# First pair's tiles, the shared block's place, the order of bc and den, and the last pair's DMAs in an attention and two-MoE kernel

## The chip, the cores and the metric

The kernel runs on one core of a Trainium2 chip. The metric is device time in microseconds (us) of one execution. A core has a matrix engine (PE), a vector engine (DVE), a scalar engine (ACT), GpSimd (POOL) and a queue engine (SP) that issues DMAs; each runs its own instructions in the order in which they stand.

## What is computed

Softmax attention with a tanh cap over 24 heads of 448 rows and 64 columns, then two feed-forward blocks on the 896 x 768 result. The weights come as 64-bit floats, the rest as 32-bit floats.

```python
scores = scale * np.matmul(q, k.transpose(0, 1, 3, 2))
scores = cap * np.tanh(scores / cap)
scores = scores - np.max(scores, axis=-1, keepdims=True)
attn = np.exp(scores)
attn = attn / (np.sum(attn, axis=-1, keepdims=True) + 1e-09)
x = np.matmul(attn, v)                      # then (B*S, H*D) = (896, 768)
h = x @ w_in;  g = np.where(h > 0.0, h, np.exp(np.minimum(h, 0.0)) - 1.0);  x = g @ w_out
h = np.maximum(x @ w_in2, 0.0);  out = h * h @ w_out2
```

## The kernel before, in words

**Pairs.** The 24 heads are worked in 12 pairs; two pairs are a group, and rows are loaded a group at a time (`load_group`: k, q, v, and "w", the last 64 rows of v). A pair's k and q are transposed on PE into one PSUM tile `pt` (`turn`, L177), which ACT copies to a rounded high part (`high`) and DVE subtracts to a low part `kql` (`low`, L189); `pt` has one buffer, so `turn(n + 2)` follows `low(n + 1)`. Every product of two matrices is then three matmuls on these parts. 448 rows are three blocks of 128 and one of 64. Scores of blocks 0 to 2 (`scores`, L230) contract over 64 rows, and the two heads run side by side in the upper and lower 64 rows of PE; block 3 of both heads is one matmul over 128 rows. ACT makes tanh (L239) and exp; `split_p` splits the result into `ph` and `pl` on DVE (L258, L259); `pv` (L281) multiplies with v, part 0 for four blocks, part 1 for the other two and, at its end, the "shared" block of the last 64 rows, whose two heads again sit in 64 rows each and which is plain 32-bit. The columns of ones beside v give the sums. `pv_out` copies the result to `pvs` (ACT, L290) and asks for the row of sums, `den` (DMA, L293). `norm` takes the reciprocal, writes it to DRAM (`far`, L305) and reads it back spread over 64 rows (`bc`, L310). `norm_x` multiplies (`xn`, L323) and splits into `xh` (L329) and `xl` (L330). The steps of one pair are spread over three turns of the loop: turn n has scores of pair n and n + 1, `pv` of n - 1 and n, `norm(n - 2)` and `norm_x(n - 3)`.

**Weights.** `Stream` turns 64-bit pieces (`wst`, five buffers) into `wf`, then `wh` and `wl`. Per piece that is an abs (ACT L385, or DVE L381 when the stream is "alone"), two DVE steps (clamp L394, shift L398), two more (sign L419, low L426, which also asks for the next piece), a copy (ACT L439, or DVE) and a subtraction (`rest`, DVE L434). `advance` interleaves the steps of two pieces. Before, pieces 0 and 1 are converted on DVE in front of the pair loop, interleaved, with piece 2 opened between; the pieces from 2 on come when the loop is done.

**The front.** `first_pair` transposes pair 0 in three pieces (k blocks 0 to 2; q; k's last block) into the one tile `pt`, with idle matmuls (`warm`, L217) between, and ACT and DVE take each piece in turn.

**The tail.** After the loop the first feed-forward matmuls (`mm_in`; b = 0 and 1 are the batches, the last pairs are b = 1) run between the last pairs' steps. `late_kc` tells how many of the 2 x 6 (k chunk, batch) steps of the first two accumulators are written ahead of the last pair's `norm_x`; the others stand behind it.

**Order.** All is written by hand (`manual_schedule`); instructions stand on their engine in the order of the code. SP issues nearly all DMAs, one after the other; an issue that waits holds up all behind it.

Of the kernel before, what the change touches and what calls it, by code (L numbers as in the profile page):

```python
# [26 lines left out]
def attention_moe_kernel(  # L27
# [133 lines left out]

    def turn(n, pieces=REST):
        if n >= len(pairs):
            return
        g, pp = divmod(n, 2)
        hs = slice(2 * pp, 2 * pp + 2)
        if ("pt", n) not in st:
            st["pt", n] = ps1.tile([P, 2, W], F32, name="pt", tag="pt")
        for u, cs in pieces:
            for c in range(NFULL + 1)[cs]:  # L170
                if c < NFULL:
                    src = nat[g]["kq"[u]][:, c, hs].rearrange("p h d -> p (h d)")
                elif u == 0:
                    src = kzs[g % 2][:, pp]
                else:
                    src = qzs[g % 2][:, hs].rearrange("p h d -> p (h d)")
                nc.tensor.transpose(st["pt", n][:, u, c * P:(c + 1) * P], src, ident)  # L177
# [15 lines left out]
    def first_pair():  # L193
        warm(5)
        cut = [(u, slice(cs.start * P, cs.stop * P)) for u, cs in FIRST]
        st["qk", 0] = [ap_.tile([P, 2, W], F32R, name=x, tag=x) for x in ("kqh", "kql")]
        h, l = st["qk", 0]
        for piece, (u, cs) in zip(FIRST, cut):
            turn(0, (piece,))
            warm(2)  # L200
            nc.scalar.copy(h[:, u, cs], st["pt", 0][:, u, cs])
            if piece is not FIRST[2]:
                nc.vector.tensor_tensor(
                    l[:, u, cs], st["pt", 0][:, u, cs], h[:, u, cs].bitcast(F32),
                    op=ALU.subtract,
                )
        u, cs = cut[2]
        nc.vector.tensor_tensor(
            l[:, u, cs], st["pt", 0][:, u, cs], h[:, u, cs].bitcast(F32), op=ALU.subtract
        )  # L210

    def warm(n):

        if "warm" not in st:
            st["warm"] = ps1.tile([P, 2, W], F32, name="po", tag="po")
# [121 lines left out]
    class Stream:  # L337
# [66 lines left out]
        def end(self, i):  # L404
# [19 lines left out]
            def low():  # L424
# [342 lines left out]
```

## Time and profile before

| what | us |
|---|---|
| median of 3 runs (611.66 to 614.39) | 612.2 |
| profiled execution, its own time | 610.04 |
| its span, first to last instruction | 608.3 |
| PE busy in the span | 587.9 (97%) |
| DVE / ACT / POOL busy | 429.1 (71%) / 334.9 (55%) / 55.7 (9%) |

The span begins at 0. Pairs run to about 138 us, the two feed-forward blocks from there to the end. PE is idle for 20 us in all, nearly all of it before 151 us. A busy time of PE is no proof that PE is at its peak: the clock that it is granted stands in a column of its own, and matmuls of one shape can be compared by how far apart they start.

### The profile page before, as it was taken

The page shows a single profiled execution, that of the slowest core. Times are in us where ns is not written, and L with a number is a line of the kernel's source. Part 1 is how long each engine was busy: PE and PEld are TensorE (multiplying, and loading weights), DVE is VectorE, ACT ScalarE, POOL GpSimd, SP SyncE. Part 2 cuts the span into 40 slices and gives each one's busy share as a digit, 9 for nine tenths or more (in the row PEclk, how much of TensorE's full clock was granted, in tenths as well). Part 3 has the DMA queues.
Part 4 walks back from the last instruction along what each step waited for, and adds up shares of the span by engine and source line. Part 5 has one row for each costly group of instructions (what it writes and reads, how often), then busy time and mean ns, then how long its engine had stood idle before and what let it go on. Part 6 is the DMA issues. An engine that isn't in the chain of part 4 may idle for free.

```text
span 608.3 us, 8606 instructions
## 1 busy us (share of the span) xinstructions
PE 587.9 (97%) x3040; PEld 526.2 (87%) x3040; DVE 429.1 (71%) x833; ACT 334.9 (55%) x484; POOL 55.7 (9%) x80
## 2 busy tenths in 40 slices
PE   7599999998999999999999999999999999999997
PEld 6477667676999999999999999999999999999997
DVE  2658999987999888676665666676777779991000
ACT  2579888852888777643333334656666655541000
POOL 3134323301000000000000000000000012130000
PEclk9799999999999999999999999999999999999999
DMA  7752441013444433333333244333334446632000
GB/s 189 192 129 68 103 111 37 28 32 109 130 133 132 126 105 96 96 112 110 99 113 121 89 128 130 105 108 118 113 107 117 108 115 188 183 92 103 23 24 35
DMA packets 82844, 64.76 MB, mean 106 GB/s; under 512 B 38512, under 2 KB 78704, under 8 KB 82800
## 3 DMA queue, kind: packets, MB, share of 16 engines
q1 hardware_dynamic: 80800, 63.74, 35.9%
q10 hardware_dynamic: 2000, 0.46, 0.3%
q8 instruction: 24, 0.39, 0.3%
q14 instruction: 20, 0.16, 0.1%
HBM read 61.34 MB, written 2.80 MB: 105 GB/s over the span
## 4 chain that ended last, share of the span: by engine, by line
PE 88%; DMA 4%; ACT 3%; DVE 2%; SPq 1%; issue 1%; ACTq 0%; POOL 0%; DVEq 0%
PE acc L497 19%; PE acc L498 19%; PE acc L496 19%; PE po L281 9%; PE acc L698 7%; PE acc L699 6%; PE acc L697 6%; PE sc L230 4%; ACT pvs L290 2%; ACT e L239 1%; DMA bc<-far 1%; DMA far<-rd 1%; DMA q<-in_q_dram 1%; DMA v<-in_v_dram 1%; DMA wst<-in_moe_w_in_dram 1%
## 5 line engine op out<-in xcount | busy, mean ns | idle before, releaser
L496 PE MATMUL acc<-xh,wh 128*128 128x448 f32 x384 | 139.9, 364 | 2.3 <-ACT xh L329 2.3
L497 PE MATMUL acc<-xl,wh 128*128 128x448 f32 x384 | 139.9, 364 | 0.2 <-DVE xl L330 0.2
L498 PE MATMUL acc<-xh,wl 128*128 128x448 f32 x384 | 139.6, 364 | 0.0
L439 ACT CAST wh<-wf 128x384 fp32r<-128x384 f32 (+2 forms) x114 | 57.9, 508 | 104.0 <-PE acc L497 85.4
L385 ACT ACTIVATE wf<-wst 128x384 f32<-128x384 f32 (+2 forms) x130 | 70.5, 543 | 62.0 <-DVE wl L434 35.1
L434 DVE TENSOR_TENSOR wl<-wf,wh 128x384 fp32r<-128x384 f32 (+2 forms) x116 | 63.7, 549 | 56.0 <-ACT wh L439 55.9
L496 PEld LDWEIGHTS acc<-xh,wh 128*128 128x128 f32 x384 | 72.1, 188 | 9.1 <-ACT xh L329 2.7
L498 PEld LDWEIGHTS acc<-xh,wl 128*128 128x128 f32 x384 | 72.1, 188 | 5.7 <-DVE wl L434 0.5
L497 PEld LDWEIGHTS acc<-xl,wh 128*128 128x128 f32 x384 | 72.1, 188 | 5.5 <-DVE xl L330 0.5
L426 DVE SCALAR_TENSOR_TENSOR wf<-wst,wf 128x384 uint32<-128x384 uint32 (+3 forms) x132 | 71.2, 540 | 0.0
L419 DVE SCALAR_TENSOR_TENSOR wf<-wst,wf 128x384 uint32<-128x384 uint32 (+3 forms) x132 | 71.2, 539 | 0.0
L497 PE MATMUL acc<-gl,wh 128*128 128x448 f32 x192 | 70.0, 365 | 0.0
L498 PE MATMUL acc<-gh,wl 128*128 128x448 f32 x192 | 70.0, 364 | 0.0
L496 PE MATMUL acc<-gh,wh 128*128 128x448 f32 x192 | 69.8, 364 | 0.0
L398 DVE TENSOR_SCALAR wf<-wf 128x384 uint32<-128x384 uint32 (+3 forms) x132 | 54.6, 414 | 0.6
L394 DVE TENSOR_SCALAR wf<-wf 128x384 f32<-128x384 f32 (+3 forms) x132 | 48.1, 364 | 7.1 <-ACT wf L385 7.1
L434 POOL TENSOR_TENSOR late<-wf,late 128x336 fp32r<-128x336 f32 x16 | 15.2, 950 | 387.9 <-ACT late L439 387.9
L239 ACT ACTIVATE e<-sc,tsc 128x896 f32<-128x896 f32 (+1 forms) x48 | 42.4, 915 | 8.8 <-PE sc L230 8.7
L684 DVE COPY o<-acc 128x432 f32<-128x432 f32 (+1 forms) x8 | 4.5, 558 | 53.9 <-PE acc L699 47.5
L698 PE MATMUL acc<-wl,gh 128*128 128x432 f32 x112 | 40.3, 359 | 0.0
L699 PE MATMUL acc<-wh,gl 128*128 128x432 f32 x112 | 40.1, 358 | 0.0
L697 PE MATMUL acc<-wh,gh 128*128 128x432 f32 x112 | 40.0, 357 | 0.0
(83 smaller groups left out, 984.0 us busy)
## 6 DMA issues: line engine op xcount, KB each, us to landing
wst<-in_moe_w_in_dram SPq DMA_DIRECT2D x64, 384.0 KB, 3.2
wst<-in_moe_w_out_dram SPq DMA_DIRECT2D x24, 384.0 KB, 3.3
wst<-in_moe_w_out_dram SPq DMA_DIRECT2D x16, 432.0 KB, 3.3
wst<-in_moe_w_out_dram SPq DMA_DIRECT2D x16, 336.0 KB, 3.0
wst<-in_moe_w_out_dram SPq DMA_DIRECT2D x12, 256.0 KB, 2.6
bc<-far SPq DMA_DIRECT2D x24, 112.0 KB, 2.8
k<-in_k_dram SPq DMA_DIRECT2D x18, 128.0 KB, 2.9
v<-in_v_dram SPq DMA_DIRECT2D x24, 96.0 KB, 2.8
```

What stands on the lines that cost most here:

```text
L281: nc.tensor.matmul(po[:, u, :S], vt[r, at[0]], pt[r, at[1]], start=i == 0 and j < 2, stop=i == 1 and j >= len(mms) - 2,)
L385: nc.scalar.activation(self.f[i], hi.bitcast(F32), AF.Abs)
L419: v.scalar_tensor_tensor(out=fb, in0=hi, scalar=0xC0000000, in1=fb, op0=ALU.bitwise_and, op1=ALU.bitwise_or,)
L426: v.scalar_tensor_tensor(out=fb, in0=lo, scalar=29, in1=fb, op0=ALU.logical_shift_right, op1=ALU.bitwise_or,)
L434: (v if dst is None else nc.gpsimd).tensor_tensor(wl, self.f[i], wh.bitcast(F32), op=ALU.subtract)
L439: (v.tensor_copy if self.alone else nc.scalar.copy)(wh, self.f[i])
L496: nc.tensor.matmul(acc, w[0], x[0], start=first, stop=False)
L497: nc.tensor.matmul(acc, w[0], x[1], start=False, stop=False)
L498: nc.tensor.matmul(acc, w[1], x[0], start=False, stop=last)
L697: nc.tensor.matmul(acc, gh[:, f, gs], w[0], start=a, stop=False)
L698: nc.tensor.matmul(acc, gh[:, f, gs], w[1], start=False, stop=False)
L699: nc.tensor.matmul(acc, gl[:, f, gs], w[0], start=False, stop=z)
```

## The change

- **The first pair.** The three pieces of pair 0 get a PSUM tile each (`pt`, `po`, and one of the two `sc`), the idle matmuls write to the other `sc`. The copies of all three pieces stand together on ACT, the subtractions on DVE, and the two small steps on `tsc` follow them. Eight idle matmuls stand in front instead of five, two behind the first piece, none behind the second and six behind the third.
- **Loads in front.** k and q of group 0 are loaded pair by pair: pair 0's first (k on SP, q on ACT), pair 1's behind them, then v of pair 0, two weight pieces, v of pair 1, and only then group 1. The first weight piece is asked for by ACT.
- **First weight pieces.** Piece 0 is converted as a whole in front of the loop (`whole`), piece 1 as a whole behind `split_p(0, 0)`.
- **The shared block** stands first in `pv` part 1.
- **bc ahead of den.** `norm(n - 2)` is written ahead of `pv_out(n - 1)`.
- **The last pair.** `start` (abs of pieces 2 and 3, clamp and shift of 2) moves into the last turn of the loop, one `advance` ahead of `split_p(11, 1)`, and the others are spread. Asking for new pieces is held (`held`) until the last `norm_x` is written. `late_kc` is 10 instead of 8. The subtraction `xl` of pairs 9 and 10 is on DVE, not POOL.

```diff
-    FIRST = ((0, slice(0, NFULL)), (1, slice(0, NFULL + 1)), (0, slice(NFULL, NFULL + 1)))
...
     def first_pair():
-        warm(5)
...
+        idle = psc.tile([P, 2, W], F32, name="sc", tag="sc")
+
+        def warm(n):
+            for _ in range(n):
+                nc.tensor.matmul(idle[:, 0, :P], ident, ident, start=True, stop=True)
+
+        qk = [ap_.tile([P, 2, W], F32R, name=x, tag=x) for x in ("kqh", "kql")]
+        st["qk", 0] = qk
+        warm(8)
+        pieces = []
+        for u, cs, pool, tag, after in (
+            (0, range(NFULL), ps1, "pt", 2),
+            (1, range(NFULL + 1), ps1, "po", 0),
+            (0, range(NFULL, NFULL + 1), psc, "sc", 6),
+        ):
+            t = pool.tile([P, 2, W], F32, name=tag, tag=tag)
+            at = slice(cs[0] * P, (cs[-1] + 1) * P)
+            for c in cs:
+                turn_one(t[:, u, c * P:(c + 1) * P], 0, u, c)
+            warm(after)
+            pieces.append((t[:, u, at], *(x[:, u, at] for x in qk)))
+        for t, h, l in pieces:
+            nc.scalar.copy(h, t)
+        for t, h, l in pieces:
+            nc.vector.tensor_tensor(l, t, h.bitcast(F32), op=ALU.subtract)
...
         if i == 1:
             shared = vss[n // 2 % 2], st["e", n]
-            mms += [(u, r, None, shared) for u, r in enumerate(ROWS)]
+            mms = [(u, r, None, shared) for u, r in enumerate(ROWS)] + mms
...
-    def norm_x(n, copy=nc.vector.tensor_copy, low=nc.gpsimd):
+    def norm_x(n, copy=nc.vector.tensor_copy):
...
-                if not self.alone:
-                    self.load()
+                self.hold += 1
+                if not (self.alone or self.held):
+                    self.release()
...
+        def release(self):
+            self.held = False
+            while self.hold:
+                self.hold -= 1
+                self.load()
...
+        def whole(self):
+
+            self.alone = True
+            self.open(self.done)
+            emit(self.begin(self.done) + self.end(self.done))
+            self.done += 1
+            self.alone = False
...
-        load_group(0, "k")
-        load_group(0, "q", dma=nc.scalar.dma_start)
+        load_group(0, "k", 0)
+        load_group(0, "q", 0, dma=nc.scalar.dma_start)
         nc.scalar.dma_start(capt, cap.unsqueeze(0).to_broadcast([P, 1]))
+        ws.load(nc.scalar.dma_start)
+        load_group(0, "kq", 1)
+        load_group(0, "vw", 0)
+        fill_kq(1, nc.gpsimd)
         ws.load()
         ws.load()
-        load_group(0, "vw", 0)
-        fill_kq(1, nc.gpsimd)
+        load_group(0, "vw", 1)
         load_group(1, "kq")
-        load_group(0, "vw", 1)
-        for _ in range(3):
-            ws.load()
+        ws.load()
+        ws.load()
         load_group(1, "vw")
...
-        emit(ws.start())
-        emit(ws.advance())
-        emit(ws.advance())
-        ws.settle()
+        ws.whole()
         for n in range(np_):
...
             turn(n + 2)
+            norm(n - 2)
+            if last:
+                emit(ws.start())
             pv_out(n - 1)
-            norm(n - 2)
...
+            if n == 0:
+                ws.whole()
             if n == 1:
-                ws.load()
-                ws.load()
+                ws.release()
...
-        late_kc = 2 * (KC - 2)
+        late_kc = 2 * (KC - 1)
+        ws.held = True
+        emit(ws.advance())
         split_p(np_ - 1, 1)
...
-        emit(norm_x(np_ - 1, nc.scalar.copy, nc.vector))
+        x, x_high, x_low = norm_x(np_ - 1, nc.scalar.copy)
+        x()
+        x_high()
+        ws.settle()
+        x_low()
+        ws.release()
```

SP at the start of the program, before. k, kz and q, qz are the full blocks and the last 64 rows of k and q (kz_90, qz_92 of group 0, kz_91, qz_93 of group 1), v and vs the same of v, wst a weight piece:

```order
L118 DMA k<-in_k_dram 128x4x64 x3
L127 DMA kz_90<-in_k_dram 64x2x64 x2
L366 DMA wst<-in_moe_w_in_dram 128x3x128 x2
L133 DMA v<-in_v_dram 128x3x64 x2
L139 DMA vs_98<-in_v_dram 64x64 x2
L118 DMA k<-in_k_dram 128x4x64 x3
L127 DMA kz_91<-in_k_dram 64x2x64 x2
L118 DMA q<-in_q_dram 128x4x64 x3
L122 DMA qz_93<-in_q_dram 64x4x64
```

The same place now:

```order
L118 DMA k<-in_k_dram 128x2x64 x3
L127 DMA kz_90<-in_k_dram 64x64 x2
L118 DMA k<-in_k_dram 128x2x64 x3
L127 DMA kz_90<-in_k_dram 64x64 x2
L118 DMA q<-in_q_dram 128x2x64 x3
L122 DMA qz_92<-in_q_dram 64x2x64
L133 DMA v<-in_v_dram 128x3x64 x2
L139 DMA vs_98<-in_v_dram 64x64 x2
L371 DMA wst<-in_moe_w_in_dram 128x3x128 x2
...
L127 DMA kz_91<-in_k_dram 64x2x64 x2
L118 DMA q<-in_q_dram 128x4x64 x3
L122 DMA qz_93<-in_q_dram 64x4x64
```

Group 1's last DMA (qz_93), for which the transposes of pair 2 wait, was the 20th that SP issues and is now the 33rd.

PE around `pv` part 1 of a pair, before (the first row is the last of block 2's scores, e with vs_98 is the shared block, the last row is the first of block 3's scores):

```order
L230 MATMUL sc<-kqh,kql 128x448 x2
L281 MATMUL po<-ph,vh_94 128x448 x2
L281 MATMUL po<-ph,vl_96 128x448 x2
L281 MATMUL po<-pl,vh_94 128x448 x2
L281 MATMUL po<-e,vs_98 128x448 x2
L230 MATMUL sc<-kqh 128x448
```

and now:

```order
L232 MATMUL sc<-kqh,kql 128x448 x2
L284 MATMUL po<-e,vs_98 128x448 x2
L284 MATMUL po<-ph,vh_94 128x448 x2
L284 MATMUL po<-ph,vl_96 128x448 x2
L284 MATMUL po<-pl,vh_94 128x448 x2
L232 MATMUL sc<-kqh 128x448
```

The shared block, of 64 rows, now follows the scores of block 2, also of 64 rows; the block-3 scores, of 128 rows, follow `pl` with vh, also of 128.

SP at the end of the pairs, before (den of the last pair, then two weight pieces, then far and bc of the last pair):

```order
L293 DMA den<-pvs 64x1x14
L366 DMA wst<-in_moe_w_in_dram 128x3x128 x2
L305 DMA far<-rd 64x14
L310 DMA bc<-far 64x448 x2
L366 DMA wst<-in_moe_w_in_dram 128x3x128 x23
```

and now:

```order
L296 DMA den<-pvs 64x1x14
L308 DMA far<-rd 64x14
L313 DMA bc<-far 64x448 x2
L371 DMA wst<-in_moe_w_in_dram 128x3x128 x25
```

The two weight pieces that stood between den and far stand behind bc.

## Rows read from the trace of the kernel before

**Rows 1.** Timeline of PE, 0 to 30 us: start, us, line, operation, [idle before <-releaser]

```profile
25.61 0.90 PE L177 MATMUL pt<-ident,k 128*128 128x128 f32 x3 [6.87 <-DVE kql L189]
...
27.50 0.74 PE L230 MATMUL sc<-kqh 64*128 64x448 f32 x2
...
28.42 0.57 PE L230 MATMUL sc<-kqh,kql 64*128 64x448 f32 x2
28.79 0.57 PE L230 MATMUL sc<-kqh 64*128 64x448 f32 x2
```

**Rows 2.** Timeline of DVE, 0 to 30 us

```profile
19.60 0.36 DVE L381 TENSOR_SCALAR wf<-wst 128x384 uint32<-128x384 uint32 x1 [6.11 <-DMA wst<-in_moe_w_in_dram]
...
24.33 1.22 DVE L189 TENSOR_TENSOR kql<-pt,kqh 128x1024 fp32r<-128x1024 f32 x1
```

**Rows 3.** Timeline of SP, 0 to 40 us

```profile
4.70 0.91 SPq L366 DMA_DIRECT2D wst<-in_moe_w_in_dram  x2
...
23.51 1.26 SPq L127 DMA_DIRECT2D kz<-in_k_dram  x2
```

**Rows 4.** Tile qz, 8 to 16 us: issue of group 1's qz to its landing

```profile
DMA to landing us min/median/max: 2.4/2.4/2.4
```

**Rows 5.** Stretches: length, busy PE, PEld, DVE, ACT, POOL (instructions), PEclk, DMA share, GB/s

```profile
23.60:30.20 6.60, 4.59 (x21) 3.54 (x21) 6.50 (x7) 1.17 (x2) 0.00 (x0) 0.50 0.63 140
30.40:37.00 6.60, 6.60 (x34) 4.71 (x34) 3.35 (x3) 4.16 (x5) 1.97 (x2) 1.00 0.17 39
100.00:120.00 20.00, 19.48 (x110) 13.68 (x109) 19.42 (x24) 17.06 (x17) 6.53 (x11) 1.00 0.10 27
```

**Rows 6.** Timeline of PE, 68.7 to 84.2 us: one pair's part 1

```profile
79.40 0.37 PE L230 MATMUL sc<-kqh,kql 64*128 64x448 f32 x2
79.70 0.67 PE L281 MATMUL po<-ph,vh 128*128 128x448 f32 x2
80.20 0.57 PE L281 MATMUL po<-ph,vl 128*128 128x448 f32 x2
80.61 0.57 PE L281 MATMUL po<-pl,vh 128*128 128x448 f32 x2
81.11 1.02 PE L281 MATMUL po<-e,vs 64*128 64x448 f32 x4
82.07 0.47 PE L230 MATMUL sc<-kqh 128*128 128x448 f32 x1
...
84.08 0.47 PE L230 MATMUL sc<-kqh 64*128 64x448 f32 x2 [0.26 <-ACT e L239]
```

**Rows 7.** Chain that ended last, 60 to 90 us: start, us, what

```profile
82.21 0.91 ACT pvs L290
83.12 0.92 ACT e L239
```

**Rows 8.** Waits of DVE, 60 to 130 us: us in total, times, longest

```profile
DVE xn L323 <- DMA bc<-far: 2.3, 5, 0.5
```

**Rows 9.** Timeline of PE, 131 to 154 us

```profile
150.36 0.47 PE L496 MATMUL acc<-xh,wh 128*128 128x448 f32 x1 [2.34 <-ACT xh L329]
151.02 0.48 PE L497 MATMUL acc<-xl,wh 128*128 128x448 f32 x1 [0.20 <-DVE xl L330]
```

**Rows 10.** Timeline of SP, 130 to 157 us

```profile
134.46 0.48 SPq L305 DMA_DIRECT2D far<-rd  x1
136.16 1.09 SPq L310 DMA_DIRECT2D bc<-far  x2
139.34 0.49 SPq L293 DMA_DIRECT2D den<-pvs  x1
139.93 1.97 SPq L366 DMA_DIRECT2D wst<-in_moe_w_in_dram  x2
142.02 0.47 SPq L305 DMA_DIRECT2D far<-rd  x1
145.48 1.09 SPq L310 DMA_DIRECT2D bc<-far  x2
```

More of the change, by code (lines that the diff above doesn't have):

```diff
@@ L153, in prep_v, with turn_one, turn @@
             nc.gpsimd.tensor_tensor(l, vn, h.bitcast(F32), op=ALU.subtract)
-    FIRST = ((0, slice(0, NFULL)), (1, slice(0, NFULL + 1)), (0, slice(NFULL, NFULL + 1)))
-    REST = ((0, slice(0, NFULL + 1)), (1, slice(0, NFULL + 1)))
-    def turn(n, pieces=REST):
+    def turn_one(to, n, u, c):
+        g, pp = divmod(n, 2)
+        hs = slice(2 * pp, 2 * pp + 2)
+        if c < NFULL:
+            src = nat[g]["kq"[u]][:, c, hs].rearrange("p h d -> p (h d)")
+        elif u == 0:
+            src = kzs[g % 2][:, pp]
+        else:
+            src = qzs[g % 2][:, hs].rearrange("p h d -> p (h d)")
+        nc.tensor.transpose(to, src, ident)
+    def turn(n):
         if n >= len(pairs):
             return
[L165 to L177, printed above, removed]
+        st["pt", n] = pt = ps1.tile([P, 2, W], F32, name="pt", tag="pt")
+        for u in range(2):
+            for c in range(NFULL + 1):
+                turn_one(pt[:, u, c * P:(c + 1) * P], n, u, c)
     def high(n):
@@ L193, in first_pair @@
     def first_pair():
-        warm(5)
[L195 to L215, printed above, removed]
-        for _ in range(n):
-            nc.tensor.matmul(st["warm"][:, 0, :P], ident, ident, start=True, stop=True)
+        idle = psc.tile([P, 2, W], F32, name="sc", tag="sc")
[21 more added lines that the diff above has]
+            nc.vector.tensor_tensor(l, t, h.bitcast(F32), op=ALU.subtract)
     def scores(n, c):
@@ L329, in norm_x @@
             lambda: copy(hi, xn),
-            lambda: low.tensor_tensor(lo, xn, hi.bitcast(F32), op=ALU.subtract),
+            lambda: nc.vector.tensor_tensor(lo, xn, hi.bitcast(F32), op=ALU.subtract),
         ]
@@ L350, in __init__ @@
             self.alone = False
+            self.hold, self.held = 0, False
         def add(self, src, a, n, keys=None, dst=None):
@@ L359, in get, with load @@
             return tuple(t[:, o] for t in self.parts[i])
-        def load(self):
+        def load(self, dma=nc.sync.dma_start):
             i = len(self.loaded)
@@ L562, in attention_moe_kernel @@
             prep_v(n + 1)
-            emit(norm_x(n - 3, low=nc.vector))
+            emit(norm_x(n - 3))
             split_p(n, 0)
@@ L594, in attention_moe_kernel @@
         emit(norm_x(np_ - 3))
-        while ws.done < 4:
-            emit(ws.advance())
+        emit(ws.advance())
         mm_in(0, 0, begun[0], xh, xl, kb[1:7:2])
```

15 lines of the change are left out of this document (6 added, 9 removed).

## The prediction

> **What bounds the kernel now.** I read the table of busy times first: PE is busy 97% of the span, so only PE's idle stretches and the time its matmuls lose can be won, and from about 151 us on PE has next to no idle time. Then the timelines of PE show where the idle time lies, and there are three places.
>
> (a) The front. PE stands 6.87 us and goes on at 25.61, released by `kql` on DVE [rows 1]. DVE had waited 6.11 us, until 19.60, for weight piece 2, then ran the rest of the conversion of pieces 0 and 1, 12 steps, up to 24.33, where `low(1)` starts [rows 2]. That is 4.73 us, 0.39 a step. A weight piece that nobody needs until the pairs are done holds up `low(1)`, and so `pt`, and so PE. Behind the idle time PE ran at half clock: 0.50 in the stretch 23.6 to 30.2, 1.00 in the next [rows 5]. Two pairs of 64-row score matmuls start 0.37 us apart there (28.42 to 28.79) [rows 1]; at full clock matmuls of the same 448 columns start 0.205 apart (80.20 to 80.61 for two) [rows 6].
>
> (b) The pairs. One pair takes about 9.2 us and its chain is PE, then ACT: when `pv` part 1 ends, ACT copies `pvs` (0.91) and makes a tanh (0.92) [rows 7], and only then has PE a free tile for the next scores; PE does block 3 and eight transposes meanwhile and still waits 0.26 [rows 6]. DVE is as full: 19.42 of 20 us [rows 5]; from 60 to 130 us it waits for nothing but `bc`, 2.3 us in all [rows 8].
>
> (c) The tail. PE waits 2.34 us for `xh` of the last pair and then starts the second matmul 0.66 behind the first instead of 0.205, so 0.46 more [rows 9].
>
> **The change part by part.**
>
> *Front loads.* `low(1)` no longer waits for piece 2: piece 0 alone, 7 steps of 0.39 = 2.7 us of DVE, stands in front, its DMA is asked for by ACT early, and piece 1 comes behind `split_p(0, 0)`, where DVE has room (3.35 busy of 6.6 in 30.4 to 37.0 [rows 5]). Without that room it would cost its 2.7 us again. What is late next is the data for pair 2's transposes, which stand in front of pair 1's scores on PE. Their last DMA, qz of group 1, was SP's 20th issue and is now the 33rd. SP's 6th issue starts at 4.70 and its 37th at 23.51 [rows 3], 18.81/31 = 0.607 us each. The 33rd starts at 4.70 + 27 x 0.607 = 21.1 and lands 2.4 later [rows 4], at 23.5; the other seven transposes can be done as their blocks land, so pair 1's scores start near 23.8, against 27.50 [rows 1]: 3.7 us earlier. The own tiles of the pieces, the earlier scores of pair 0 and the changed idle matmuls bring nothing by themselves: all of it is over before 23.5 and lies beside SP's issuing. Were the loads not the limit, they would be worth more; so their cost is 0, with SP's queue as the cover.
>
> The clock takes part of it back. PE stands idle again before 23.5, so I expect half clock again. If full clock comes back at the same time as before, about 30.3, there are 3.7 us more at half clock, in which PE does 0.205/0.37 = 0.55 of the work: 1.65 lost, gain 2.05. If half clock lasts as long after the burst's start as before (25.61 to 30.3), the gain is the whole 3.7. If it lasts a second stretch like 23.6 to 30.2, PE is at half clock for 11 us instead of 2.8 behind the first scores, 8.2 x 0.45 = 3.7 is lost, and the gain is 0. I take **2.0** (the first, since nothing moves the clock's change by itself), bounds 0 and 3.7.
>
> *Shared block.* From 64-row to 128-row matmuls the start-to-start time is 0.30 (79.40 to 79.70) instead of 0.205, and the next two take 0.50 (79.70 to 80.20) instead of 0.41: 0.10 + 0.09, so a change of shape costs about 0.2 us. Before, part 1 had three: scores to `ph`, `pl` to shared (80.61 to 81.11, again 0.50 for two), shared to block 3 (81.11 to 82.07) [rows 6]. Now one is left, shared to `ph`. Of the two that go, one lies on the chain; the other lies between the end of part 1 and the next scores, where PE waits for ACT anyway: it turns into idle time, 0.26 growing to about 0.45. So 0.2 a pair. It holds for the first 11 pairs; the last has other 128-row matmuls around it, two changes before and two now. 11 x 0.2 = 2.2 us.
>
> *DVE and bc.* A faster pair needs a faster DVE. `far` and `bc` no longer queue behind `den`, which waits for ACT's `pvs`, so I expect the 2.3 us of waits [rows 8] to go. `den` now queues behind `far` and `bc`, and behind `den` the loads of k, q and v; its only reader is the reciprocal of the next turn, some 9 us on, so this costs 0; the cover is that turn. In the last turn DVE gets clamp and shift of piece 2, 2 x 0.39 = 0.8, ahead of `split_p(11, 0)`. DVE's room to pair 11 is therefore 2.3 - 0.8 = 1.5, and the 0.4 from the first two pairs, when DVE still waits for ACT: 1.9, less than PE's 2.2. I take **1.9**; bounds 0.5 (the `bc` waits stay in part) and 4.4 (both changes of shape count, 22 x 0.2).
>
> *Last pair's DMAs.* Before, SP issued `den` at 139.34, then two weight pieces until 139.93 + 1.97 = 141.90, then `far` at 142.02; `bc` could go only at 145.48, 3.46 later, while a pair earlier it took 136.16 - 134.46 = 1.70 with no weight piece on the way [rows 10]. Without them `far` can go when the reciprocal is there, at 139.34 + about 1.8 for `den` + 0.3 = 141.4 (1.8 is an estimate from that 1.70, the same kind of small DMA). That is 0.6 + 1.76 = 2.4 earlier, so `xh` at 150.36 - 2.4 = 148.0. PE's work lasted to 150.36 - 2.34 = 148.0, and three matmuls more (`late_kc`) stand in front of the wait, 3 x 0.205 = 0.6, so the wait of 2.34 goes, and most of the 0.46. The steps of piece 2 that now stand ahead of `split_p(11, 1)` lie where DVE waits for exp, and the two `xl` moved to DVE (about 0.5 each, an estimate from 0.39 for 384 columns) lie beside PE's 48 matmuls; uncovered they would cost 1.0. The held weight pieces (7 to 9) land some us later than before; PE needs pieces 4, 5 and 6 first, which are long there, so this costs 0; if it did not hold, PE would wait for `wl` behind the tail. I take **2.6**; bounds 1.2 (`far` as slow as before, only the queue's 0.6 and the three matmuls' 0.6) and 3.3.
>
> **Sum.** 2.0 + 1.9 + 2.6 = 6.5 us. Against the profiled execution's 610.04 that is 603.5; the median of the runs shown lies 2.2 above it, and by the median it is 605.7. I take the middle of the two, 611.1 - 6.5 = **604.6**.
>
> **The rivals.**
> - *Group 1's rows come late.* For it: 13 more issues stand ahead of qz. Against it: the same 0.607 held over 31 issues of all kinds. At 0.74 each qz lands at 27.1, PE starts as before, the gain is 4.5: 606.6. Chance 0.10.
> - *The clock.* The stretch of idle time in front of pair 1's scores is as long as before or longer, and half clock could last through a second stretch: front 0, 606.6. Chance 0.10. The Trainium skill, TensorE: Matmul & The Clock Gate, section "HAM oscillation — how this bites in real kernels", says that a gap between bursts sets PE back to half clock and that this is paid again at each gap; by that rule the front's half clock stays whatever the loads do, and the trace agrees with its 0.50 [rows 5]. The page also has the moment of the change vary from run to run, which would let this rival and the full 3.7 both occur.
> - *The change of shape stays.* Scores are in the rounded format and the shared block is plain 32-bit; no row shows these two side by side in 64 rows. If that change costs the 0.2 that I take out, the pairs gain nothing: 606.5. Chance 0.08. The Trainium skill, TensorEngine Tiling, section "Key Properties", ties the drain to the tiling mode ("Changing tiling mode (not just tile) drains the TensorE"), which speaks against this rival; no run so far shows this pair.
> - *DVE becomes the bound.* It is 97% busy; if `bc` keeps coming late, PE waits for `ph` and `pl` and the pairs give 0.5: 606.0. Chance 0.08.
> - *It doesn't do what it says in the tail.* `far` takes 3.4 us for another reason than the weight pieces: tail 1.2, 606.0. Chance 0.05.
> - *Slower.* SP's front queue is the place, 1 us for each us is the price. If qz of group 1 lands after 27.2, PE starts later than before; slower than before from 27.2 + 4.5 = 31.7, at (31.7 - 2.4 - 4.70)/27 = 0.91 us an issue. At 1.1 it lands at 36.8, and the time is 611.1 + 5.1 = 616.2. For it: many small transfers at once; against it: 0.607 was measured with the DMA engines as full. Chance 0.04.
>
> **How the numbers follow.** The forecast has 0.55, the rivals 0.45 together. A measurement of this kernel can tell about 0.5%, 3.1 us, so faster means under 609.1. Each rival alone but the last stays under it; two or three together don't, for which I count 0.12. Faster 0.84, same 0.12, slower 0.04. The range: the bounds of the three terms give gains from 1.7 to 11.4, but the ends need all three; two terms at the low end and one at its value give 2.0 + 0.5 + 1.2 = 3.7 or less, against the median 608.5; at the high end 3.7 + 1.9 + 3.3 = 8.9 against the profiled 610.04, 601.1.
>
> **What would show it.** Right: no wait of DVE for a weight piece in the first 25 us, PE's transposes of pair 2 released by a DMA near 23.5; pairs of about 9.0 us with 0.30 only behind the shared block and PE's wait for tanh near 0.45; no waits of `xn` for `bc`; `far` to `bc` 1.7 us for the last pair and no wait of PE for `xh` over 0.5. Wrong: qz landing behind 25, half clock beyond 31, the shared block starting 0.30 behind the scores, PE waiting for `ph` or `pl` in each pair, or new waits of PE for `wl` behind 150.

## The result and the profile after

The changed kernel takes 604.49 us (median of 4 runs, 603.58 to 605.78) against 611.93 for the kernel before (4 runs, 610.03 to 614.39): a ratio of 0.9878, 95% interval 0.9838 to 0.9918, so the gain is clear of the noise. The profiled execution took 605.78, its span is 604.0. The forecast was 604.6. PE is busy 582.4 us (96%), DVE 429.7, ACT 334.9, POOL 62.1.

**Front.** PE after, 12 to 36.6 us (start, us, line, operation, [idle before <-releaser]); these answer [rows 1]:

```profile
17.81 1.37 PE L167 MATMUL pt<-ident,k 128*128 128x128 f32 x3 [4.96 <-DMA k<-in_k_dram]
...
24.82 0.45 PE L167 MATMUL pt<-ident,qz 128*128 128x128 f32 x1 [2.16 <-DMA qz<-in_q_dram]
25.20 0.74 PE L232 MATMUL sc<-kqh 64*128 64x448 f32 x2
...
35.95 0.47 PE L232 MATMUL sc<-kqh 64*128 64x448 f32 x2 [0.42 <-ACT e L241]
```

SP after, 15 to 23 us, which answers [rows 3]:

```profile
19.80 0.61 SPq L122 DMA_DIRECT2D qz<-in_q_dram  x1
20.45 1.13 SPq L371 DMA_DIRECT2D wst<-in_moe_w_in_dram  x2
```

The tile qz after, 18 to 26 us, which answers [rows 4]:

```profile
DMA to landing us min/median/max: 4.9/4.9/4.9
```

DVE no longer stands in the way; the rows of group 1 do. qz is issued at 19.80 and lands 4.9 us later, at 24.7, so pair 1's scores begin at 25.20, 2.3 us earlier than before. Pair 2's begin at 35.95, against 37.96 before: a lead of 2.0.

Stretches after (columns as in [rows 5], which they answer):

```profile
17.00:25.00 8.00, 3.35 (x8) 1.46 (x8) 5.55 (x10) 0.00 (x0) 1.97 (x4) 0.50 0.81 203
25.20:29.20 4.00, 4.00 (x17) 3.16 (x17) 0.53 (x1) 2.47 (x3) 0.00 (x0) 0.51 0.76 175
29.40:36.00 6.60, 6.18 (x38) 4.69 (x36) 2.66 (x3) 3.87 (x5) 2.01 (x2) 1.00 0.63 143
...
127.20:131.60 4.40, 4.40 (x14) 3.94 (x15) 4.33 (x7) 1.67 (x3) 0.00 (x0) 0.61 0.00 0
```

PE ran at 0.50 (1.2 GHz) from 17 to 29 us, behind its 4.96 us of idle time, and a second time behind 127.2 us, where before had 1.00.

**Pairs.** PE after, 66 to 81.5 us, one pair's part 1, which answers [rows 6]:

```profile
71.94 0.47 PE L232 MATMUL sc<-kqh 64*128 64x448 f32 x2 [0.42 <-ACT e L241]
...
76.50 0.37 PE L232 MATMUL sc<-kqh,kql 64*128 64x448 f32 x2
76.70 0.92 PE L284 MATMUL po<-e,vs 64*128 64x448 f32 x4
77.55 0.67 PE L284 MATMUL po<-ph,vh 128*128 128x448 f32 x2
78.06 0.57 PE L284 MATMUL po<-ph,vl 128*128 128x448 f32 x2
78.47 0.57 PE L284 MATMUL po<-pl,vh 128*128 128x448 f32 x2
78.88 0.36 PE L232 MATMUL sc<-kqh 128*128 128x448 f32 x1
...
80.94 0.47 PE L232 MATMUL sc<-kqh 64*128 64x448 f32 x2 [0.42 <-ACT e L241]
```

The shared block starts 0.20 behind the scores (76.50 to 76.70), block 3 starts 0.41 behind `pl` for two matmuls, and the period is 80.94 - 71.94 = 9.00 (9.19 to 9.30 before, one pair 9.53).

Waits of DVE after, 60 to 130 us (total, times, longest), which answer [rows 8]:

```profile
DVE wf L399 <- ACT wf L390: 1.2, 1, 1.2
```

The waits for `bc` are gone, and a new one is there.

**Tail.** DVE after, 121 to 131 us:

```profile
122.99 0.36 DVE L399 TENSOR_SCALAR wf<-wf 128x384 f32<-128x384 f32 x1 [1.24 <-ACT wf L390]
123.38 0.36 DVE L403 TENSOR_SCALAR wf<-wf 128x384 uint32<-128x384 uint32 x1
...
125.93 1.08 DVE L260 CAST ph<-e 128x1792 fp32r<-128x1792 f32 x1
```

ACT after, 116 to 128 us:

```profile
120.73 1.79 ACT L249 ACTIVATE e<-e,capt 128x1792 f32<-128x1792 f32 x1
122.43 0.97 ACT L390 ACTIVATE wf<-wst 128x384 f32<-128x384 f32 x2
```

PE after, 120 to 153 us, which answers [rows 9]:

```profile
127.16 1.05 PE L284 MATMUL po<-ph,vh 128*128 128x448 f32 x4 [2.48 <-DVE ph L260]
128.05 1.64 PE L284 MATMUL po<-ph,vl 128*128 128x448 f32 x4
```

PE before, 118 to 131 us, the same matmuls:

```profile
129.71 1.04 PE L281 MATMUL po<-ph,vh 128*128 128x448 f32 x4 [0.28 <-ACT pvs L290]
```

SP after, 128 to 152 us, which answers [rows 10]:

```profile
138.34 0.51 SPq L296 DMA_DIRECT2D den<-pvs  x1
140.43 0.46 SPq L308 DMA_DIRECT2D far<-rd  x1
142.09 1.09 SPq L313 DMA_DIRECT2D bc<-far  x2
```

`start`, now in the last turn, puts clamp and shift of piece 2 ahead of the last pair's split on DVE. The clamp waits for ACT's abs, and the abs stands behind an exp of 1.79 us. So `ph` is 2 us late, PE idles 2.48 us instead of 0.28, and half clock follows it (0.61). The last pair's DMAs did what they should: `far` to `bc` takes 142.09 - 140.43 = 1.66 (3.46 before), and PE's wait of 2.34 for `xh` is gone.

From the 101st matmul of the feed-forward blocks on, all kernels below take 446.6 us to the end of PE's last matmul. So what sets them apart lies in the first 155 us, and this table follows it. Medians are us; the ratio is against the kernel before, run beside it on the same chip; then three starts from the profiled execution.

| kernel | median | ratio (95%) | profiled, own time | pair 2's first scores | pair 4's block 2 | pair 11's first scores |
|---|---|---|---|---|---|---|
| before | 611.93 | | 610.04 | 37.96 | 60.44 | 121.33 |
| after | 604.49 | 0.9878 (0.9838-0.9918) | 605.78 | 35.95 | 57.99 | 116.97 |
| e1_start_late | 603.70 | 0.9859 (0.9834-0.9884) | 603.48 | 34.97 | 57.02 | 115.96 |
| e2_shared_only | 610.18 | 0.9970 (0.9944-0.9996) | 610.93 | 37.99 | 60.06 | 120.22 |
| e3_bc_first | 611.90 | 0.9983 (0.9964-1.0002) | 609.64 | 37.59 | 60.16 | 120.82 |
| e4_front_only | 608.76 | 0.9945 (0.9925-0.9965) | 609.94 | 35.52 | 58.01 | 119.29 |
| e5_tail_only | 608.03 | 0.9949 (0.9930-0.9969) | 608.98 | 38.86 | 62.08 | 122.93 |
| e6_group1_early | 605.68 | 0.9902 (0.9870-0.9933) | 605.64 | 30.81 | 58.59 | 118.13 |
| e7_turn2_late | 604.78 | 0.9896 (0.9861-0.9932) | 603.65 | 29.81 | 57.38 | 116.36 |
| e8_warm | 603.59 | 0.9876 (0.9846-0.9905) | 603.42 | 33.19 | 57.19 | 116.31 |
| e9_shared_and_bc | 608.60 | 0.9944 (0.9924-0.9965) | 608.66 | 38.35 | 60.41 | 119.40 |
| e10_warm_less_sp | 602.55 | 0.9841 (0.9816-0.9866) | 602.60 | 33.45 | 55.50 | 115.56 |
| e11_front_anew | 601.95 | 0.9830 (0.9805-0.9856) | 602.51 | 32.74 | 55.01 | 115.06 |
| e12_front_again | 600.31 | 0.9796 (0.9780-0.9812) | 600.31 | 26.66 | 54.38 | 113.37 |

e1 to e4 ran on one chip (before: 611.82 there), e5 to e8 on another (611.18), e9 to e11 on a third (611.50), e12 on a fourth (612.35). A start read from one trace is good to about 1 us only: at pair 2, kernels whose front is that of before lie between 37.59 and 38.86, and the changed kernel and e1, whose fronts are the same, at 35.95 and 34.97. What the expectations of e8 to e12 call "pair 5's scores" at 51 to 57 us is block 2 of pair 4, the column above.

### The profile page after: what moved, and what is told of

Read it like the earlier page. It is cut to its first block, busy times and chain, and to the rows that moved or that the text cites. A ratio compares the mean times of both kernels' runs of the same rounds, so it can differ in the third digit from the quotient of the medians.

```text
span 604.0 us, 8619 instructions
## 1 busy us (share of the span) xinstructions
PE 582.4 (96%) x3044; PEld 527.4 (87%) x3044; DVE 429.7 (71%) x835; ACT 334.9 (55%) x484; POOL 62.1 (10%) x78
## 4 chain that ended last, share of the span: by engine, by line
PE 89%; ACT 4%; SPq 2%; DMA 2%; issue 1%; DVE 1%; ACTq 0%
PE acc L516 19%; PE acc L517 19%; PE acc L515 19%; PE po L284 9%; PE acc L724 7%; PE acc L725 6%; PE acc L723 6%; PE sc L232 4%; ACT e L241 2%; ACT pvs L293 2%; SPq L118 1%; DMA qz<-in_q_dram 1%; DMA q<-in_q_dram 0%; DMA bc<-far 0%; SPq L127 0%
## 5 line engine op out<-in xcount | busy, mean ns | idle before, releaser
L399 DVE TENSOR_SCALAR wf<-wf 128x384 f32<-128x384 f32 (+3 forms) x132 | 46.8, 354 | 8.5 <-ACT wf L390 8.4
L710 DVE COPY o<-acc 128x432 f32<-128x432 f32 (+1 forms) x8 | 4.5, 558 | 53.8 <-PE acc L725 47.7
```

## Each part alone

**e2_shared_only: the kernel before with the shared block first.**

```diff
-            mms += [(u, r, None, shared) for u, r in enumerate(ROWS)]
+            mms = [(u, r, None, shared) for u, r in enumerate(ROWS)] + mms
```

> The kernel before with the shared block first in pv part 1, nothing else. Theory A (one change of shape of 0.2 us goes from each pair's chain): pairs of 9.0 us where DVE keeps up, the wait for tanh 0.42 instead of 0.26, time 1.5 to 2.2 us under before. Theory B (DVE, with its late bc, takes over): pairs over 9.1 us from the sixth on, PE waits for ph or pl, time under 1 us better.

Measured: 1.64 us off the median; from pair 2 to pair 11 82.23 us instead of 83.37, 1.14 less. Most pairs are 9.00 apart, two are 9.3 and 9.9. DVE of e2, 89 to 97 us, at such a pair:

```profile
89.98 1.30 DVE L323 TENSOR_TENSOR xn<-pvs,bc 64x448 f32<-64x448 f32 x2 [0.75 <-DMA bc<-far]
...
92.59 1.48 DVE L258 CAST ph<-e 128x1792 fp32r<-128x1792 f32 x1
```

and PE of e2, 92 to 96 us:

```profile
94.22 1.06 PE L281 MATMUL po<-ph,vh 128*128 128x448 f32 x4 [0.43 <-DVE ph L258]
```

The late `bc` reaches PE through DVE, as the forecast's cap on this term had it.

**e3_bc_first: `norm(n - 2)` ahead of `pv_out(n - 1)` in the kernel before, nothing else.**

```diff
-            pv_out(n - 1)
             norm(n - 2)
+            pv_out(n - 1)
```

> The kernel before with norm(n - 2) written ahead of pv_out(n - 1), nothing else. Theory A (bc was late because far queued behind den): DVE's waits of xn for bc between 60 and 130 us fall from 2.3 us to under 0.5, but PE gains only the one long pair, 0.3 us: no difference that can be measured. Theory B (the late bc costs more, since DVE is as full as PE): 1 us or more.

Measured: 0.08 over its neighbours' median, 83.23 us from pair 2 to pair 11, 0.14 less than before. DVE's waits for `bc` are gone, and PE had not been waiting for DVE.

**e9_shared_and_bc: both edits.**

> The kernel before with two parts together: the shared block first in pv and bc asked for ahead of den. Theory (the shared block takes 0.2 us out of every pair, but only if DVE, which waits for bc, is let go too; so the two are worth more together than the sum of each alone): pairs 9.00 us apart as in the changed kernel, 2.0 to 2.4 us earlier at the last pair's scores than before, median 2 to 2.8 us under before (608.5 to 609.5). Rival (the two add up as measured alone, 1.64 and near 0): some pairs 9.3 us and longer as in e2_shared_only, at the last pair's scores 1.1 to 1.5 us ahead of before, median 1.3 to 1.9 us under before.

Measured: 2.90 us off the median, 0.1 more than the theory's 2 to 2.8, and 81.05 us from pair 2 to pair 11, 2.32 less than before, against 1.14 + 0.14 for the two apart. All pairs are 9.0 apart and DVE waits for no DMA from 60 to 130 us. The theory holds: the second edit is worth nothing until the first makes DVE the next thing late.

**e4_front_only: the changed front, with `start` at the end of turn 1, and the pairs and tail of before** (against the changed kernel):

```diff
-            mms = [(u, r, None, shared) for u, r in enumerate(ROWS)] + mms
+            mms += [(u, r, None, shared) for u, r in enumerate(ROWS)]
...
             if n == 1:
                 ws.release()
+                emit(ws.start())
...
-        late_kc = 2 * (KC - 1)
+        late_kc = 2 * (KC - 2)
...
```

> The changed front alone: loads, first pair and weight pieces 0 and 1 as in the changed kernel, with shared block, den and bc and the tail as before (abs of pieces 2 and 3 in the second turn). Theory A (pair 1's scores start when qz of group 1 has landed): they start at 24 to 25.5 instead of 27.5, PE is about 2 us ahead at 36 us, time 1.5 to 2.5 us under before, tail wait 2.3 us as before. Theory B (the front's gain is the clock's, which changes from run to run): the lead at 36 us differs from 2 by over 1 us.

Measured: 3.06 us off the median, more than the 1.5 to 2.5 expected, and pair 2's scores 2.4 earlier. At pair 11's first scores 2.0 of it are left; at the end of the tail nothing is, in the profiled execution. About 0.6 is gone by the end of the wait for `xh` (PE waits 0.5 for `ph` and 0.2 for `pl` ahead of it); most of the rest is the clock. PE of e4, 146 to 154 us:

```profile
148.93 0.58 PE L515 MATMUL acc<-xh,wh 128*128 128x448 f32 x1 [2.42 <-ACT xh L332]
```

The stretch behind it in e4 (columns as in [rows 5]):

```profile
148.90:152.40 3.50, 3.39 (x9) 2.70 (x10) 3.49 (x9) 1.07 (x2) 0.00 (x0) 0.54 0.02 5
```

Before's profile had the same wait of 2.34 [rows 9] and clock 1.00 behind it, e3 and e9 (2.57, 2.70) too; e2 and e4 fell to 0.57 and 0.54 (1.2 GHz for nearly all of it) for some 3.5 us. Nine matmuls instead of before's 15 went through in that time, 6 x 0.20 = 1.2 us lost. That would be part of why the runs of before spread from 609.5 to 614.6. Their traces are not there to count it, but each run's mean granted clock is: of e3's ten runs, the five at 0.986 took 612.1 to 612.7, the five at 0.988 and more 608.9 to 611.7. Where in a run the clock fell, that figure doesn't tell.

**e5_tail_only: the kernel before with the tail's parts (held loads, `late_kc`, the order of the steps, `norm_x` on DVE), without `start` in the last turn.**

```diff
-        late_kc = 2 * (KC - 2)
+        late_kc = 2 * (KC - 1)
+        ws.held = True
+        emit(ws.advance())
         split_p(np_ - 1, 1)
...
```

> The kernel before with the tail alone changed: weight pieces held back and issued at the end, the last pair's norm on VectorE, three more product steps of the first two sums ahead of the wait for xh, and no start() in the last turn. Theory (the tail's term of 2.6 us was right, and the changed kernel lost it to the clamp that start() put ahead of the split of e): PE's wait of 2.34 us for xh goes, the products on the last weight pieces begin 2.3 to 2.9 us earlier in the trace than before, and the median falls by 2 to 3.5 us to 608.5 to 610, the upper end of the gain being runs of before in which the wait is followed by half clock. Rival (the last pair's DMAs were not late because of other DMAs, or the held pieces come too late): the wait for xh stays over 1 us or a wait for a weight piece of the same size takes its place, and the median stays within 1 us of before.

Measured: 3.15 us off the median. PE of e5, 144 to 156 us:

```profile
149.43 0.37 PE L507 MATMUL acc<-xh,wl 128*128 128x448 f32 x1
149.86 0.47 PE L505 MATMUL acc<-xh,wh 128*128 128x448 f32 x1
150.52 0.48 PE L506 MATMUL acc<-xl,wh 128*128 128x448 f32 x1 [0.19 <-DVE xl L330]
```

No wait for `xh` is left. From pair 11's first scores to the 151st product matmul it takes 44.44 us against 47.11: 2.67 less, where the forecast had 2.6. End to end this trace shows only 1.07 of it, since it comes to pair 4 already 1.6 us late: DVE waits 1.9 us there for `bc`, in a part of the kernel that the edit leaves alone.

**e1_start_late: the changed kernel with `start` behind `split_p(11, 0)`.**

```diff
-            if last:
-                emit(ws.start())
             pv_out(n - 1)
...
             split_p(n, 0)
+            if last:
+                emit(ws.start())
```

> The changed kernel, but the abs, clamp and shift of weight pieces 2 and 3 in the last turn stand behind split_p(11, 0) instead of ahead of norm_x(8). Theory A (DVE's wait for ACT's abs delays split_p and so pv(11, 0), and PE's idle time there brings half clock): PE's wait at pv(11, 0) falls from 2.48 to 0.3 to 0.6 us, the half-clock stretch near 128 to 131 goes, and the profiled span is 3 to 3.5 us under a profile of the changed kernel with the same clock in front, 600 to 601. Theory B (DVE is simply full in the last pairs): the wait stays above 1.5 us and the span moves by under 1 us.

Measured: 603.70, 0.8 under the changed kernel's median, its four runs within 0.6 us; the two intervals overlap. The profiled span is 601.7, not the 600 to 601 expected, and 1.0 us of its 2.3 under the changed kernel's comes from the front, which the edit leaves alone. PE of e1, 118 to 146 us:

```profile
124.12 1.05 PE L284 MATMUL po<-ph,vh 128*128 128x448 f32 x4 [0.44 <-ACT pvs L293]
...
138.02 0.47 PE L517 MATMUL acc<-xh,wl 128*128 128x448 f32 x1 [0.77 <-DVE wl L440]
...
144.42 0.47 PE L515 MATMUL acc<-xh,wh 128*128 128x448 f32 x1 [0.40 <-ACT xh L332]
```

The wait of 2.48 is 0.44 now, and the clock stays at 1.00 from 124 to 131.6. But the same stretch as above takes 45.97 us, against 47.27 in the changed kernel and 47.11 before: 1.14 less than before and not 2.67. Piece 2's first steps are still in the tail, and PE now waits 0.77 for its `wl`. e5 had them done in front of the loop.

## What bounds the front

**e6_group1_early: e1 with group 1's k and q ahead of pair 1's v and two weight pieces.**

```diff
+        load_group(1, "kq")
+        load_group(0, "vw", 1)
         ws.load()
         ws.load()
-        load_group(0, "vw", 1)
-        load_group(1, "kq")
```

> The kernel of e1_start_late with group 1's k and q asked for right behind the first pair's v, ahead of pair 1's v and of two weight pieces: six issues on SP, and 0.79 MB of weights, fewer in front of it. Theory (PE's idle stretch from 12.3 to 23.5 us is the wait for group 1's rows, and their landing goes by SP's issues and what is queued ahead): qz is issued at about 16.2 us instead of 19.7 and lands at 18.5 to 20; pair 1's scores begin at 19 to 20.5 instead of 23.6, pair 2's at 31.5 to 33 instead of 35.0, since some of it is paid back at half clock; median 600.5 to 602.5. Rival (something else is late right behind it, pair 1's v above all, now issued 4 us later): pair 2's scores no more than 0.7 us earlier, median within 0.8 us of 603.7.

Measured: 605.68, by the median 2.0 above e1 (on another chip, and the two intervals overlap a little), so no gain, though pair 2's scores came 4.2 us earlier (30.81). DVE of e6, 44 to 56 us:

```profile
50.25 0.23 DVE L306 RECIPROCAL rd<-den 64x14 f32<-64x14 f32 x1 [5.25 <-DMA den<-pvs]
...
52.61 1.09 DVE L260 CAST ph<-e 128x1792 fp32r<-128x1792 f32 x1
```

SP of e6, 33 to 52 us:

```profile
34.04 0.52 SPq L296 DMA_DIRECT2D den<-pvs  x1
34.66 1.06 SPq L371 DMA_DIRECT2D wst<-in_moe_w_in_dram  x2
35.82 1.54 SPq L118 DMA_DIRECT2D k<-in_k_dram  x3
...
46.62 1.12 SPq L313 DMA_DIRECT2D bc<-far  x2
47.83 0.55 SPq L296 DMA_DIRECT2D den<-pvs  x1
```

PE then waits 3.55 us for that `ph`, and runs at half clock for most of 53.8 to 60.6 (0.55). Between the first pair's `den` and the second's stand two weight pieces, all of a group's k, q and last rows of v, and `far` and `bc` of the first pair, issued one behind the other but for the 2.5 us in which `bc` waits for `far`. So the second comes at 47.83, in e7 at 47.22, in e8 at 47.78, in e1 at 46.32, whatever PE does. DVE's reciprocal waits for it, and the next split stands behind the reciprocal. Part of this queue is the change's own: it put `far` and `bc` of the first pair ahead of that `den`. In e4, which has the changed front but `den` ahead of `far` and `bc`, it went at 44.22, 2.1 to 3.6 us before these four. SP of e4, 30 to 56 us:

```profile
44.22 0.56 SPq L296 DMA_DIRECT2D den<-pvs  x1
```

No run has a faster front with that order.

**e7_turn2_late: e1 with pair 2's transposes behind pair 0's first half of `pv`.**

```diff
-            turn(n + 2)
+            if n:
+                turn(n + 2)
...
             pv(n, 0)
+            if not n:
+                turn(2)
```

> The kernel of e1_start_late with pair 2's transposes moved on TensorE from ahead of pair 1's first scores to behind pair 0's first half of pv; loads as in e1_start_late. Theory (the place of these transposes, not the loads, makes PE idle): pair 1's first scores begin at 14.5 to 15.5 us, the idle stretch shrinks from 11 us to under 7 us, and since ScalarE's copy of pair 2's kq still stands ahead of pair 1's second tanh, pair 2's scores come 1.5 to 3 us earlier than 35.0; median 600.5 to 602.5. Rival (the rows' landing at 23 us sets everything behind it): pair 2's scores within 0.7 us of 35.0 and median within 0.8 us of 603.7.

Measured: 604.78, no gain. Pair 2's scores come 5.2 us earlier than in e1, more than the theory had, but pair 4's block 2 comes at 57.38 against 57.02. Waits of PE in e7, 36 to 62 us, the first row:

```profile
PE po L284 <- DVE ph L260: 4.0, 1, 4.0
```

DVE waits 5.7 us for the same `den` there.

**e8_warm: e1 with 46 idle matmuls in PE's idle stretch.**

```diff
+            if not n:
+                busy = ps1.tile([P, 2, W], F32, name="po", tag="po")
+                for _ in range(46):
+                    nc.tensor.matmul(busy[:, 0, :P], ident, ident, start=True, stop=True)
             turn(n + 2)
```

> The kernel of e1_start_late with 46 idle 128x128 matmuls on PE ahead of pair 2's transposes, which fill its wait from 12.3 to 17.8 us and are read by nothing. Theory (half of the front's gain is eaten by the half clock that follows this wait): the granted clock stays 1.00 through the transposes and pair 1's first scores, pair 2's scores begin at 32.5 to 34 instead of 35.0, median 601.5 to 603. Rival (the waits of 2 us in the transposes between 17.8 and 23.2 bring half clock by themselves, or DVE and ACT, not PE, set pair 2's start): clock 0.50 from about 21 us on and pair 2's scores within 0.7 us of 35.0, median within 0.8 us of 603.7.

Measured: 603.59, no gain. Stretches of e8 (columns as in [rows 5]):

```profile
17.00:25.00 8.00, 7.55 (x68) 7.19 (x68) 5.32 (x9) 0.00 (x0) 2.33 (x4) 1.00 0.78 198
25.00:33.00 8.00, 7.76 (x47) 5.82 (x43) 3.15 (x3) 6.29 (x6) 1.77 (x2) 1.00 0.79 184
```

PE of e8, 32 to 34 us, pair 2's first scores:

```profile
33.19 0.47 PE L232 MATMUL sc<-kqh 64*128 64x448 f32 x2 [0.42 <-ACT e L241]
```

With full clock throughout, pair 1's first scores and pair 2's are 33.19 - 24.16 = 9.03 us apart; in e1, at half clock up to about 29.0, it is 34.97 - 23.56 = 11.41. The half clock costs 2.38 there, and by the forecast's 0.45 for each us at half clock 5.4 x 0.45 = 2.4. The gain is given back at 54 us, in a wait of 1.51 for `ph` behind `den` (2.92 on DVE). So three different ways to make PE faster in front end at pair 4's block 2 at 57.2 to 58.6, against e1's 57.0 and the changed kernel's 58.0: in all three the wait for that `den` sets the point. In the changed kernel it landed at 49.48 and the reciprocal started at 50.04, so 0.56 us were left.

**e10_warm_less_sp: e8 with five weight pieces taken out of SP's stream of the front and asked for in turns 3 to 7.**

```diff
         ws.load()
-        ws.load()
         load_group(0, "vw", 1)
         load_group(1, "kq")
-        ws.load()
-        ws.load()
...
             if n == 1:
-                ws.release()
+                ws.hold = 0
+            if 3 <= n < 8:
+                ws.load()
```

> The kernel of e8_warm with three weight pieces fewer asked for on SP in the front and the two of the second turn taken out too; all five are asked for one by one in turns 3 to 7. Theory (in e6, e7 and e8 the front's lead was given back at pair 5, where DVE's reciprocal waits for den, which stands on SP behind the whole stream of loads; SP, not PE, sets pair 5 as soon as the front gains more than 1 us over e1): SP comes to that den about 2.5 us earlier, the wait of 2.92 us on DVE at 50 us and that of 1.51 us on PE at 54 us go, pair 5's scores begin at 53.5 to 55.5 instead of 57.2, median 600.5 to 602.5. Rival (the den's landing goes by far and bc and not by SP's backlog): the wait of PE for ph at 54 us stays over 1 us, pair 5's scores at 56.5 or later, median within 0.8 us of 603.6.

Measured: 602.55. Waits of DVE in e10, 36 to 62 us, all of them:

```profile
DVE ph L260 <- ACT e L249: 3.4, 3, 1.5
```

No wait for `den`, and pair 4's block 2 at 55.50, 1.69 earlier than in e8. The theory holds. Its `den` left SP at 44.65, 3.1 us earlier than in e8. One microsecond was lost again at 85 us, where a `den` comes 1.00 late; e1 has no such wait.

**e11_front_anew and e12_front_again: the versions that follow.** e11 is e1 with the edits of e6 and e7, the weight pieces moved as in e10 and ACT's copy of pair 2 behind pair 1's exp:

```diff
-            if n:
+            if n > 1:
                 high(n + 1)
...
             exp(n, 0)
+            if n == 1:
+                high(n + 1)
             low(n + 1)
...
```

> The kernel of e1_start_late with the three front changes together: group 1's k and q ahead of pair 1's v, pair 2's transposes behind pair 0's first half of pv (and ScalarE's copy of them behind pair 1's exp), and four weight pieces out of SP's stream of the front, asked for in turns 3 to 7. Theory (the front is bound by SP's stream of issues, and what each of e6 and e7 gained was lost to it): pair 1's scores at 14.5 to 15.5 us, pair 2's at 26 to 29 instead of 35.0, pair 5's at 51.5 to 55 instead of 57.0, median 597.5 to 601.5. Rival (den and the loads still set pair 5): a wait of 2 us and more for ph or for pair 4's rows between 40 and 60 us, pair 5's scores at 56 or later, median 602.5 to 604.5.

Measured: 601.95. Pair 2's scores come at 32.7 instead of 26 to 29; DVE of e11, 16 to 31 us, says why:

```profile
23.46 0.36 DVE L386 TENSOR_SCALAR wf<-wst 128x384 uint32<-128x384 uint32 x1 [6.37 <-DMA wst<-in_moe_w_in_dram]
```

The weight piece that I had put last on SP held up the split behind it, the very fault that the change had taken out of the kernel before [rows 2].

e12 cuts the unpacking of the second weight piece in two and puts it at the ends of turns 1 and 2, asks for the later pieces in turns 3, 5, 7 and 9, and fills PE's first wait with 18 idle matmuls (against e11):

```diff
+            if not n:
+                busy = ps1.tile([P, 2, W], F32, name="po", tag="po")
+                for _ in range(18):
+                    nc.tensor.matmul(busy[:, 0, :P], ident, ident, start=True, stop=True)
...
-            if n == 0:
-                ws.whole()
             if n == 1:
+                ws.alone = True
+                ws.open(1)
+                emit(ws.begin(1))
+                ws.alone = False
+            if n == 2:
+                ws.alone = True
+                emit(ws.end(1))
+                ws.alone = False
+                ws.done += 1
                 ws.hold = 0
-            if 3 <= n < 8:
+            for _ in range({3: 1, 5: 1, 7: 1, 9: 2}.get(n, 0)):
+                ws.load()
```

> The kernel of e11_front_anew with its two new waits taken away and its first idle stretch filled: VectorE's unpacking of the second weight piece, which waited 6.37 us for that piece's load at 23.5 us and held up the second half of pair 0's split, is cut in two and stands at the ends of turns 1 and 2; the five pieces asked for later are issued in turns 3, 5, 7 and 9, not right ahead of far; 18 idle matmuls, read by nothing, fill PE's wait of 2.24 us ahead of pair 1's scores. Theory (those two waits are all that is left between e11 and the steady period): no wait of PE over 1 us between 13 and 60 us, the clock 1.00 throughout, pair 2's scores at 26.5 to 29.5 instead of 32.7, all later pairs 9.00 us apart without the long one at 87 us, median 596.5 to 599.5. Rival (SP's stream of issues is late again for den or for group 2's rows): a wait of PE over 1.5 us between 30 and 60 us, the lead at the last pair's scores under 1.5 us over e11, median 600.5 to 602.5.

Measured: 600.31 (598.16 to 600.73), above the theory's 596.5 to 599.5 but the best of all: ratio 0.9796, its interval clear of the changed kernel's. PE of e12, 12 to 27 us:

```profile
26.66 0.47 PE L232 MATMUL sc<-kqh 64*128 64x448 f32 x2 [0.42 <-ACT e L241]
```

Waits of DVE in e12, 36 to 62 us:

```profile
DVE rd L306 <- DMA den<-pvs: 6.4, 2, 4.0
```

Pair 2's scores come 8.3 us earlier than in e1, with the clock at 1.00 from 13 to 44 us, but pair 11's only 2.6: the reciprocals wait 6.4 us for `den`, and PE 2.98 us behind the second of them. That is the rival's mechanism, a little cheaper than it was priced (1.69 over e11 at pair 11's first scores, where the rival had under 1.5). The front now waits for SP's `den`, not for PE.

## Why the prediction was right, step by step

The sum of 6.5 us came out (604.6 against 604.49), but not all of its terms did. In the two traces the lead is 2.0 in front, 2.35 in the pairs (4.36 at pair 11's first scores) and -0.16 in the tail, 4.2 together (the 2.0 holds the 0.2 that the shared block gives the first pair). The medians differ by 7.4, since before's profiled execution was as fast as its fastest run (1.9 under the median) and after's its slowest (1.3 over). So it is luck that the forecast came within 0.1: from before's profile it was 603.5, against 605.78 in the changed kernel's; from the median it was 605.7, against 604.49.

- **SP's 0.607 us an issue and qz as the 33rd issue: right, the start of the count taken 1.0 too late.** Predicted at 21.1, it went at 19.80: the sixth issue started at 3.72 instead of 4.70, and the 27 up to qz took 0.596 each.
- **Landing 2.4 us later: wrong.** 4.9 in this trace, so pair 1's scores came at 25.20, not 23.8; in e1 and e4, with the same front, it was 3.3. The row [rows 4] was of one qz; before's next one took 3.6. Why it varies stays open.
- **Half clock up to about 30.3: near.** It ended at about 29.1, an error of 1.2 us the other way. So the 2.0 in front (1.8 without the shared block's 0.2) came out because three errors cancel, which is luck. The price, 0.45 for each us at half clock, held in e8 (2.38 against 2.4).
- **The shared block, 0.2 a pair, one of two changes of shape on the chain: right.** The wait for tanh went from 0.26 to 0.42 (0.45 said). The rival that the format matters fell: 0.20 from scores to the shared block. The Trainium skill, TensorEngine Tiling (Array Packing), section "Key Properties", ties the drain to a change of tiling mode; the trace agrees, 0.10 and 0.09 at a change of rows and nothing at a change of format alone.
- **DVE as the limit of the pairs: that a late `bc` reaches PE through DVE was right (e2, e3, e9), the cap of 1.9 too low.** Measured 2.35. I had taken 0.8 for clamp and shift out of DVE's room in this term; they hurt only in the tail. DVE, busy 52.6 of the 54 us from 60 to 114 and waiting for no DMA, did not keep the pairs from 9.00.
- **`den` behind `far` and `bc`, priced at 0: right here** (DVE has no wait for it from 36 to 130 us), but the cover of a turn was down to 0.56 us at the second `den`, and it is what e6, e7, e8 and e12 ran into.
- **`far`, `bc` and three matmuls in the tail, 2.6: right alone** (2.67 in e5's trace, 3.15 in its median), **and lost in the changed kernel.** The step that failed is "DVE gets clamp and shift of piece 2, 0.8". It priced two instructions by their length and not by what the first waits for: ACT's abs behind exp, 1.24 us of waiting, so that PE idled 2.48 instead of 0.28. The half clock that followed is counted in no term. Moving `start` (e1) ends both, and gives back 1.30 of the 2.83 us that the tail takes longer than e5's.
- **No cost of the held pieces: right.** No wait of PE for a weight piece in the changed kernel's tail.
- **The clock rival** (a second half-clock stretch in front) did not come; the stretch that came was in the tail.

By medians the parts alone are worth 3.06 (e4) + 2.90 (e9) + 3.15 (e5) = 9.1, the whole 7.4. The intervals are about 1.2 us to either side for each part and 2.4 for the whole, so that difference alone shows nothing; the traces of the tail do. e1, without `start`'s wait, has 8.1 on its chip. Its tail still takes 1.53 longer than e5's; its waits of 0.77 for `wl` (piece 2's conversion) and 0.40 for `xh` fit most of that, but no run took them out of it, so it stays open. Open too is how much of the medians of e5 and the changed kernel is half clock behind `xh` that some runs of before have.

## What to carry to other kernels

Price a moved instruction by the engine that it waits for, not by its own length: here 0.7 us of VectorE work cost 2.2 us of TensorE and a stretch at half clock. Before speeding up an engine, find the next queue that sets the same point (here SP's stream of issues); three edits that gave PE 2 to 5 us in front were worth nothing while loads that nobody needed yet stood in that queue. An edit that is worth nothing alone can be worth something beside another (`bc` ahead of `den`: 0.14 us alone, 1.18 behind the shared block's 1.14), so test the pair before dropping one.

## What the runs showed of the hardware

- **The same gap, two clocks.** Behind waits of 2.34, 2.57 and 2.70 us for `xh` the granted clock stayed at 1.00 (2.4 GHz) in before, e3 and e9; in e2, e4 and the changed kernel, behind waits of 2.42 to 2.48, it was 0.54 to 0.61 over the next 3.5 to 4.4 us. The Trainium skill, TensorE: Matmul & The Clock Gate, section "HAM oscillation — how this bites in real kernels", says that a long enough wait between bursts sets PE back to half clock; waits of this length did so in three of these traces and not in the other three (before, e3, e9). No row here tells what decides it.
- **The same small transfer lands after 2.4 to 4.9 us.** Group 1's qz landed 3.3 to 4.9 us after its issue in the five kernels with two weight pieces of 384 KB right behind it (after, e1, e4, e7, e8), and 2.4 to 2.9 in the nine with other loads behind it. But group 2's qz, with only v behind it, took 3.6, 4.5 and 4.2 in before, e5 and e9, so that the pieces behind it are the cause is not shown.
- **Idle matmuls kept the clock in e8.** With 46 of them, read by nothing, it was 1.00 from 17 to 25 us, where e1 had 0.50.
